# Sign of float64 weight slices from a Prelu on ScalarE, fp32r products in the first unit, and a new order, in an mLSTM-and-MLP kernel

## The chip, the cores and the metric

The kernel runs on one core of a Trainium2 chip. Its engines run side by side, each through its own queue in program order, and wait for one another by semaphores: TensorE (PE; its weight loads are PEld) multiplies into PSUM, VectorE (DVE) and ScalarE (ACT) do elementwise work, GpSimd (POOL) does a little of that on SBUF alone, and SyncE (SP) issues the DMAs. The metric is the device time of the program in microseconds, the median of several runs.

## The reference

Two stages. The first is a recurrent attention over 768 steps for 4 batches of 8 heads of width 40, with exponential gates that are kept stable by a running maximum `m`:

```
m_new  = max(f_t + m, i_t)
f_stab = exp(f_t + m - m_new);  i_stab = exp(i_t - m_new)
C = f_stab*C + i_stab * (v_t k_t^T)      # 40 x 40 per head
n = f_stab*n + i_stab * k_t
y_t = sigmoid(o_t) * (C q_t) / max(|n . q_t|, 1)
```

The second takes the 3072 x 320 result as `x`:

```
h = x @ w_in                     # 320 x 2048, float64
g = h * clip(h + 3, 0, 6) / 6
out = (g @ w_out) as float32     # 2048 x 320, float64
```

The weights come as float64, the rest as float32, and the result is float32.

## The kernel before

**Stages.** The recurrence is computed in chunks of 128 steps: inside a chunk it is a masked product of q, k and v, and between chunks a 40 x 40 state `C` is carried. Six chunks of 4 batches make 24 rows of 128 tokens; three of them are a unit, and eight units follow one another. A unit has two tasks (four heads each) of three chunks. Per chunk there are these jobs: `gate` (the matrix `gw` of gate weights: its first seven made by TensorE products `gb`, the others by a DMA from a scratch tensor and a masking on GpSimd, then four exponentials on ScalarE), `front` (scores `s`, times `gw` on VectorE, and the state's update), `back` (product `o` with v), and per task `fin` (division, output gate, transpose into `xh` and `xl`, the high and low part of x in fp32r). Then the unit's MLP: 16 slices `f` of 128 hidden columns. For each, `mm1` makes `h` by eight fp32r products, ScalarE and VectorE make `g`, and for each pair of slices `mm2` adds to three output tiles `acc`.

**Precision.** For units u >= NV, `g` is split into `gh` (cast on ScalarE, through the helper line L403) and `gl` (the rest, VectorE, L918), and the output weights into `vh` and `vl`, so that `mm2` makes three fp32r products per slice and tile (L937 to L939). Unit 0 (u < NV = 1) uses the whole fp32 `g` and the whole fp32 weight `vr` in one product (L935), which the profile shows as two instructions. For tasks >= PT = 6, `front` splits the weighted scores into three bf16 parts `p` (cast, subtract, cast, subtract) and `split_v` does so with v (`vb`), and `back` makes 16 bf16 products; the tasks before that use fp32 (L741).

**The weights.** The float64 words arrive as pairs of 32-bit words, eight slices of `w_in` (`rawi`) and eight of `w_out` (`rawo`). `weight_slice` makes the float32 value of each: ScalarE scales the high word, read as a float32, by 2^-112 (L824) and turns the low word into three bits (L826); then there are three operations on `y`, the clamp (L829), a shift with an OR of the low word's bits (L831), and an AND that takes the sign bit of the high word with an OR (L836). For `w_in`, `whi`, `wlo` and `wtl` are then split off for `mm1`. `split_out` makes `vh` and `vl`; it is set off for each slice by an `mm2` step of unit 0.

**The order.** Nothing is left to a run-time scheduler. A planner written in the kernel (class `Plan`) plays the jobs against a table of costs and due times, and writes each engine's queue in the order that it finds. The constants at the top are its due times and offsets (SPAN, T0, AH, EV, EG, MV, G0 to G2, ...), its cost corrections (BA, BD, BG) and buffer counts. `ENGINES` is a string with a letter for each of 28 choices: d, a or p for VectorE, ScalarE or GpSimd alone, x for VectorE or GpSimd, y for VectorE or ScalarE, z for all three. GP gives the groups of chunks in which the gates are computed, FC chooses how `fin` of unit 0 is cut. Until the `mm1` buffers are opened, the job `warm` puts filler products `pw` (128 x 128 bf16 of zeros) into TensorE's queue wherever the work of the last 3.41 us of the plan is below RATE columns.

Of the kernel before, what the change touches and what calls it, by code (L numbers as in the profile page):

```python
# [7 lines left out]
F32 = mybir.dt.float32  # L8
# [3 lines left out]
AF = mybir.ActivationFunctionType  # L12
ALU = mybir.AluOpType
# [18 lines left out]
MS = 1  # L32
BKO = 9.255
CHANGE = {"moe": 0.085, ("moe", "front"): 0.092, ("moe", "state"): 0.092, ("back", "front"): 0.085, ("fin", "front"): 0.095, ("back", "state"): 0.085, ("fin", "state"): 0.095, ("front", "moe"): 0.105, ("state", "moe"): 0.106}
STICK = 39.626
NGW = 3
NPT = 2
W_DOWN = 2.0**-112
W_MAX = 2.0**-96 * (1.875 - 2.0**-23)
W_LOW = 0.9374 * 2.0**-29  # L40
PT = 6
GB = 7
NV = 1
NY = 3
NRAW = 3
SPAN = 69.454
T0 = 103.209
AH = 21.763
GP = [1, 2, 3]
G0 = -113.271  # L50
G1 = -53.152
G2 = 54.685
AH1 = 87.929
FC = 1
FCS = {2: [[(0, 2)], [(0, 1), (1, 1)]], 3: [[(0, 3)], [(0, 2), (2, 1)], [(0, 1), (1, 1), (2, 1)], [(0, 1), (1, 2)]], 1: [[(0, 1)], [(0, 1)]]}
LON = 4.789
WAI = -1.158
WAO = -18.316
WAS = 151.09
MV = -6.903  # L60
DELTA = -1.652
EGW = 1
EV = 99.864
EG = 59.663
HOP = 0.167
# [280 lines left out]
def mlstm_moe_kernel(ctx: ExitStack, tc: tile.TileContext, ig, fg, qkd, natd, ond, w_in, w_out, ident_d, out):  # L346
    nc = tc.nc
# [18 lines left out]
    VR, VH, VL = {}, {}, {}  # L366
# [31 lines left out]
    def E(c):  # L398
        return {"d": nc.vector, "g": nc.gpsimd}[c]
# [413 lines left out]
    def weight_slice(kind, i, n):  # L813
# [9 lines left out]
        yield "a", 0.73  # L823
        nc.scalar.activation(w, hw.bitcast(F32), AF.Copy, scale=W_DOWN)  # L824
# [4 lines left out]
        E(e).tensor_scalar(w, w, W_MAX, -W_MAX, ALU.min, ALU.max)  # L829
        yield "d", Lock(0.765)  # L830
        nc.vector.scalar_tensor_tensor(lw, y, 3, lw, ALU.logical_shift_left, ALU.bitwise_or)  # L831
# [271 lines left out]
```

## Time and profile before

| | |
|---|---|
| median of 3 runs | 505.31 us (505.13 to 507.19) |
| the profiled execution | 505.4 us, span 503.7 us |
| granted TensorE clock | 0.999 |
| PE busy | 494.5 us (98%) |
| DVE busy | 356.1 us (71%) |
| ACT busy | 262.3 us (52%) |
| POOL busy | 95.2 us (19%) |
| first `h` product | 50.54 us |

A row of the profile names the line, the engine, the operation and the tiles as out<-in; "x128" is the number of instructions, then come their busy time and the mean duration of one in ns. In rows in order of time the first column is the start in us and the second the length. Matmuls are pipelined, and their durations overlap: what one costs is the distance between two starts, not its length. Line numbers after L403 differ by one or two between the two kernels, since one line was added at the top and two were taken out of `weight_slice`.

### The profile page before, as it was taken

How to read it: one execution, taken by the hardware profiler on the slowest of the kernel's cores; microseconds unless marked ns; L12 is line 12 of the kernel's file. 1: busy time of each engine (PE TensorE's matmuls, PEld its weight loads, DVE VectorE, ACT ScalarE, POOL GpSimd, SP SyncE). 2: the span in 40 equal slices, each digit the busy share in tenths (PEclk: the TensorE clock that was granted, in tenths of full speed). 3: DMA queues.
4: the chain of work that ended last, by engine and by line, in shares of the span. 5: the costliest groups of instructions: out<-in, count | busy, mean ns of one | idle time of the engine just before them, and what ended most of it. 6: DMA issues, size and time to landing. Idle time of an engine off the chain costs nothing.

```text
span 503.7 us, 10688 instructions
## 1 busy us (share of the span) xinstructions
PE 494.5 (98%) x4199; PEld 465.3 (92%) x4199; DVE 356.1 (71%) x839; ACT 262.3 (52%) x606; POOL 95.2 (19%) x117
## 2 busy tenths in 40 slices
PE   8999999999999999999999999999999999999997
PEld 7998787889999999999999999999899999999997
DVE  7998898976556676766877677777878777753332
ACT  4866758644456554555545554644545552343333
POOL 3213001001011141421233132421223131000000
PEclk9999999999999999999999999999999999999999
DMA  8757865514232231324131441324140230001001
GB/s 280 254 157 222 298 187 190 165 44 142 64 104 83 69 116 51 116 82 135 46 108 43 116 122 52 115 92 123 42 122 25 81 101 2 1 1 40 1 0 40
DMA packets 24610, 50.79 MB, mean 101 GB/s; under 512 B 2544, under 2 KB 9008, under 8 KB 24560
## 3 DMA queue, kind: packets, MB, share of 16 engines
q1 hardware_dynamic: 24560, 50.11, 31.8%
q8 instruction: 33, 0.54, 0.5%
q14 instruction: 17, 0.14, 0.1%
HBM read 46.07 MB, written 4.03 MB: 99 GB/s over the span
## 4 chain that ended last, share of the span: by engine, by line
PE 82%; DVE 5%; DMA 5%; ACT 3%; POOL 2%; issue 1%; POOLq 0%; SPq 0%; ACTq 0%; DVEq 0%
PE h L894 31%; PE acc L937 9%; PE acc L939 9%; PE acc L938 9%; PE s L693 5%; DMA gw<-gsc 5%; PE acc L935 4%; PE o L741 3%; PE s L696 3%; PE s L610 2%; PE x L798 2%; PE pw L424 1%; ACT gw L666 1%; PE o L743 1%; PE gb L654 1%
## 5 line engine op out<-in xcount | busy, mean ns | idle before, releaser
L908 ACT ACTIVATE g<-h,half 128x384 f32<-128x384 f32 x128 | 73.7, 576 | 109.3 <-PE h L894 101.9
L910 DVE SCALAR_TENSOR_TENSOR g<-g,h 128x384 f32<-128x384 f32 x128 | 70.6, 551 | 75.3 <-ACT g L908 74.7
L937 PE MATMUL acc<-vh,gh 128*128 128x320 f32 x336 | 106.9, 318 | 0.0
L939 PE MATMUL acc<-vh,gl 128*128 128x320 f32 x336 | 104.0, 309 | 0.0
L938 PE MATMUL acc<-vl,gh 128*128 128x320 f32 x336 | 103.9, 309 | 0.0
L894 PE MATMUL h<-xh,whi 128*128 128x384 f32 x256 | 92.3, 361 | 0.6 <-DVE g L910 0.5
L894 PE MATMUL h<-xh,wlo 128*128 128x384 f32 x256 | 86.5, 338 | 0.0
L894 PE MATMUL h<-xl,whi 128*128 128x384 f32 x256 | 86.4, 338 | 0.0
L918 DVE TENSOR_TENSOR gl<-g,gh 128x384 fp32r<-128x384 f32 x112 | 66.1, 593 | 20.9 <-ACT gh L403 19.6
L403 ACT CAST gh<-g 128x384 fp32r<-128x384 f32 x112 | 57.1, 510 | 44.0 <-DVE g L910 43.7
L666 ACT ACTIVATE gw<-gw,cT 128x128 f32<-128x128 f32 x164 | 54.2, 392 | 43.2 <-POOL gw L660 43.1
L660 POOL TENSOR_SCALAR_AFFINE_SELECT gw<-gw 128x512 f32<-128x512 f32 x41 | 29.4, 716 | 209.1 <-DMA gw<-gsc 140.9
L937 PEld LDWEIGHTS acc<-vh,gh 128*128 128x128 f32 x336 | 63.1, 188 | 0.5
L938 PEld LDWEIGHTS acc<-vl,gh 128*128 128x128 f32 x336 | 63.2, 188 | 0.0
L939 PEld LDWEIGHTS acc<-vh,gl 128*128 128x128 f32 x336 | 63.1, 188 | 0.0
L894 PEld LDWEIGHTS h<-xh,whi 128*128 128x128 f32 x256 | 48.1, 188 | 4.4 <-DVE g L910 2.8
L719 POOL TENSOR_TENSOR gw<-gw,p 128x512 f32<-128x512 f32 x30 | 35.0, 1166 | 85.7 <-DVE p L405 80.0
L894 PEld LDWEIGHTS h<-xl,whi 128*128 128x128 f32 x256 | 48.2, 188 | 0.6
L894 PEld LDWEIGHTS h<-xh,wlo 128*128 128x128 f32 x256 | 48.1, 188 | 0.0
L894 PE MATMUL h<-xh,wtl 128*128 128x384 f32 x128 | 43.3, 338 | 0.0
L894 PE MATMUL h<-xl,wtl 128*128 128x384 f32 x128 | 43.2, 337 | 0.0
L701 DVE TENSOR_TENSOR gw<-s,gw 128x512 f32<-128x512 f32 x48 | 32.9, 687 | 7.2 <-PE s L696 6.4
(112 smaller groups left out, 818.9 us busy)
## 6 DMA issues: line engine op xcount, KB each, us to landing
st<-in_qk_dram SPq DMA_DIRECT2D x48, 256.0 KB, 3.5
gw<-gsc SPq DMA_DIRECT2D x41, 256.0 KB, 3.3
nat<-in_nat_dram SPq DMA_DIRECT2D x16, 492.0 KB, 4.5
rawi<-in_w_in_dram SPq DMA_DIRECT2D x8, 640.0 KB, 6.4
rawo<-in_w_out_dram SPq DMA_DIRECT2D x8, 640.0 KB, 4.9
on<-in_on_dram SPq DMA_DIRECT2D x8, 480.0 KB, 4.5
out_dram<-ob SPq DMA_DIRECT2D x24, 160.0 KB, 1.8
f_s<-in_fg_dram SPq DMA_DIRECT2D x1, 96.0 KB, 2.2
```

The lines of the kernel that those rows point to most:

```text
L403: nc.scalar.copy(dst, src)
L660: nc.gpsimd.affine_select(gw, gw, pattern=[[0, 4], [1, L]], compare_op=ALU.is_ge, fill=NEG, base=0, channel_multiplier=-1)
L666: nc.scalar.activation(gw[:, h, :], src[:, h, :], AF.Exp, bias=cT[:, c, r0 + h : r0 + h + 1], scale=1.0)
L701: nc.vector.tensor_tensor(gw.rearrange("p (z j) l -> p z (j l)", z=2), sp[:, :, : 2 * L], gw.rearrange("p (z j) l -> p z (j l)", z=2), ALU ...
L719: E(e).tensor_sub(gw, gw, p[:, 0])
L894: nc.tensor.matmul(hp, w, x, start=n == 0, stop=n == len(seq) - 1)
L908: nc.scalar.activation(g, hp, AF.Relu, bias=half, scale=1.0 / 6.0)
L910: nc.vector.scalar_tensor_tensor(g, g, 1.0, hp, ALU.min, ALU.mult)
L918: E(e).tensor_sub(gl, g, gh.bitcast(F32))
L937: nc.tensor.matmul(acc, gh[:, ts_], VH[f // 4][:, f % 4, :], start=f == 0, stop=False)
L938: nc.tensor.matmul(acc, gh[:, ts_], VL[p][:, f % 2, :], start=False, stop=False)
L939: nc.tensor.matmul(acc, gl[:, ts_], VH[f // 4][:, f % 4, :], start=False, stop=f == NF - 1)
```

## The change

ScalarE's Copy of the high word becomes a Prelu with slope 2^32 for negative inputs. A negative weight then comes out 2^32 times as large in magnitude. That adds 32 to the exponent field, which is the bit 2^28 of the word, and the shift by 3 that follows anyway carries it into the sign bit. So the separate operation that fetched the sign (L836) is gone; the shift with OR writes the final tile, and the clamp has an asymmetric lower bound.

The constants: NV 1 to 0 (unit 0 uses the split fp32r form too, and `split_out` runs as soon as a slice of `w_out` is done), PT 6 to 4 (unit 2's tasks use the bf16 split), GP [1, 2, 3] to [1, 2, 1, 2], FC 1 to 0 (`fin` of unit 0 in one step of three chunks a task instead of two steps), RATE 4500 to 3690, and new due times. In ENGINES, among others, the subtractions of `p` and of v (23), the casts of `whi` (24) and the products `vp` (6) get other choices.

```diff
@@ constants
-BKO = 9.255
+BKO = 5.044
-STICK = 39.626
+STICK = 49.917
+W_SIGN = 2.0**32
-PT = 6
+PT = 4
-NV = 1
+NV = 0
-SPAN = 69.454
-T0 = 103.209
-AH = 21.763
-GP = [1, 2, 3]
+SPAN = 70.624
+T0 = 123.535
+AH = 19.252
+GP = [1, 2, 1, 2]
...
-FC = 1
+FC = 0
...
-RATE = 4500
+RATE = 3689.588
...
-ENGINES = 'ddpdddzxdaddxdddxxdaaaapaadx'
+ENGINES = 'dxpxadzddadddxddxxdaaaaxdapx'
@@ weight_slice
-        nc.scalar.activation(w, hw.bitcast(F32), AF.Copy, scale=W_DOWN)
+        nc.scalar.activation(w, hw.bitcast(F32), AF.Prelu, scale=W_DOWN, alpha=W_SIGN)
         yield "a", 0.73
         nc.scalar.activation(lw, lw, AF.Copy, scale=W_LOW)
         plan.now["t"] -= 0.73
         e = yield pick(14, d=Lock(0.46), g=1.0)
-        E(e).tensor_scalar(w, w, W_MAX, -W_MAX, ALU.min, ALU.max)
-        yield "d", Lock(0.765)
-        nc.vector.scalar_tensor_tensor(lw, y, 3, lw, ALU.logical_shift_left, ALU.bitwise_or)
+        E(e).tensor_scalar(w, w, W_MAX, -W_MAX * W_SIGN, ALU.min, ALU.max)
         fs = slice(i * 256, (i + 1) * 256)
         if kind == "o":
             VR[i] = wts.tile([128, 2, DM], U32, tag=f"vl{i}", bufs=1, name=f"vr{i}")
         yield "d", Lock(0.765)
-        nc.vector.scalar_tensor_tensor(VR[i].rearrange("p a d -> p (a d)") if kind == "o" else y, hw, 0x80000000, lw, ALU.bitwise_and, ALU.bitwise_or)
+        nc.vector.scalar_tensor_tensor(VR[i].rearrange("p a d -> p (a d)") if kind == "o" else y, y, 3, lw, ALU.logical_shift_left, ALU.bitwise_or)
```

Three places show how the queues move. The first is VectorE in the head of the program, from the first weight slice's clamp on (`yi` and `rawi` are the slice's tiles; the number after a name tells instances apart). Before:

```order
L829 TENSOR_SCALAR yi_166<-yi_166 128x640
L491 COPY cT<-pc_304 128x96
L831 SCALAR_TENSOR_TENSOR rawi_111<-yi_166,rawi_111 128x640
L495 COPY gTs<-pc_304 128x96
L836 SCALAR_TENSOR_TENSOR yi_166<-rawi_111 128x640
L577 TENSOR_TENSOR vp_146<-nat_107,wT 128x168
L829 TENSOR_SCALAR yi_175<-yi_175 128x640
L831 SCALAR_TENSOR_TENSOR rawi_112<-yi_175,rawi_112 128x640
```

Now:

```order
L830 TENSOR_SCALAR yi_166<-yi_166 128x640
L406 COPY ht_159<-o_0_312 128x168
L505 TENSOR_TENSOR wT<-pc_279,cT 128x32
L835 SCALAR_TENSOR_TENSOR yi_166<-yi_166,rawi_111 128x640
L492 COPY cT<-pc_336 128x64
L578 TENSOR_TENSOR vp_151<-nat_108,wT 128x168
L496 COPY gTs<-pc_336 128x64
L578 TENSOR_TENSOR vp_151<-nat_108,wT 128x168
L406 CAST whi<-yi_166 128x2x256
L578 TENSOR_TENSOR vp_369<-nat_150,wT 128x168
L830 TENSOR_SCALAR yi_175<-yi_175 128x640
```

One operation on 640 words stands after the clamp instead of two, and the `vp` products (GpSimd's before, but for one) and the cast of `whi` (ScalarE's before) have come into VectorE's queue.

The second is TensorE in unit 0, where the first `mm2` step begins. Before:

```order
L894 MATMUL h_2_1001<-xh_502,wtl 128x384
L894 MATMUL h_2_1001<-xl_503,wtl 128x384
L935 MATMUL acc_0_1029<-vr_660,g_0_974 128x320
L935 MATMUL acc_0_1029<-vr_660,g_1_997 128x320
L935 MATMUL acc_1_1036<-vr_660,g_0_974 128x320
L935 MATMUL acc_1_1036<-vr_660,g_1_997 128x320
L935 MATMUL acc_2_1045<-vr_660,g_0_974 128x320
L935 MATMUL acc_2_1045<-vr_660,g_1_997 128x320
L894 MATMUL h_3_1030<-xh_502,whi 128x384
```

Now, the first third of the step:

```order
L893 MATMUL h_4_964<-xh_540,wtl 128x384
L893 MATMUL h_4_964<-xl_541,wtl 128x384
L936 MATMUL acc_0_988<-vh_795,gh_0_865 128x320
L937 MATMUL acc_0_988<-vl_796,gh_0_865 128x320
L938 MATMUL acc_0_988<-vh_795,gl_0_866 128x320
L936 MATMUL acc_0_988<-vh_795,gh_1_915 128x320
L937 MATMUL acc_0_988<-vl_796,gh_1_915 128x320
L938 MATMUL acc_0_988<-vh_795,gl_1_916 128x320
L936 MATMUL acc_1_1006<-vh_795,gh_0_865 128x320
```

Three products take the place of one, and two more slices of `h` (up to 4 instead of 2) stand ahead of the first step.

The third is a chunk's split while unit 3's MLP runs (the first chunk of unit 4's second task). VectorE before:

```order
L405 COPY C_0_3253<-s_0_3183 128x84
L787 TENSOR_TENSOR on_2907<-on_2907,rd_0_3199 128x3x160
L405 CAST p_0_3263<-gw_0_2887 128x512
L910 SCALAR_TENSOR_TENSOR g_4_3247<-g_4_3247,h_4_3185 128x384
L918 TENSOR_TENSOR gl_4_3249<-g_4_3247,gh_4_3248 128x384
L804 TENSOR_TENSOR xl_3198<-x_8_0_3266,xh_3197 128x384
L405 CAST p_0_3263<-gw_0_2887 128x512
L723 TENSOR_TENSOR p_0_3263<-gw_0_2887,p_0_3263 128x512
L910 SCALAR_TENSOR_TENSOR g_5_3298<-g_5_3298,h_5_3246 128x384
```

VectorE now:

```order
L406 COPY C_0_3374<-s_0_3341 128x84
L406 CAST p_0_3442<-gw_0_3061 128x512
L720 TENSOR_TENSOR gw_0_3061<-gw_0_3061,p_0_3442 128x512
L406 CAST p_0_3442<-gw_0_3061 128x512
L805 TENSOR_TENSOR xl_3344<-x_8_0_3433,xh_3343 128x384
L724 TENSOR_TENSOR p_0_3442<-gw_0_3061,p_0_3442 128x512
L406 COPY ht_3340<-o_0_3464 128x168
L909 SCALAR_TENSOR_TENSOR g_5_3476<-g_5_3476,h_5_3404 128x384
```

The subtraction between the two casts of `p` (L720; L719 before) stood in GpSimd's queue and stands in VectorE's now, so the split no longer leaves that engine; in GpSimd's new queue, behind the gates' four subtractions, there is nothing but the maskings of `gw`.

More of the change, by code (lines that the diff above doesn't have):

```diff
@@ L39 @@
 W_MAX = 2.0**-96 * (1.875 - 2.0**-23)
+W_SIGN = 2.0**32
 W_LOW = 0.9374 * 2.0**-29
-PT = 6
+PT = 4
 GB = 7
-NV = 1
+NV = 0
 NY = 3
 NRAW = 3
-SPAN = 69.454
-T0 = 103.209
-AH = 21.763
-GP = [1, 2, 3]
[L50 to L53, printed above, removed]
-FC = 1
-FCS = {2: [[(0, 2)], [(0, 1), (1, 1)]], 3: [[(0, 3)], [(0, 2), (2, 1)], [(0, 1), (1, 1), (2, 1)], [(0, 1), (1, 2)]], 1: [[(0, 1)], [(0, 1)]]}
[L56 to L61, printed above, removed]
+SPAN = 70.624
+T0 = 123.535
+AH = 19.252
+GP = [1, 2, 1, 2]
+G0 = -120.578
+G1 = -25.639
+G2 = 24.583
+AH1 = 73.471
+FC = 0
+FCS = {2: [[(0, 2)], [(0, 1), (1, 1)]], 3: [[(0, 3)], [(0, 2), (2, 1)], [(0, 1), (1, 1), (2, 1)], [(0, 1), (1, 2)]], 1: [[(0, 1)], [(0, 1)]]}
+LON = -2.289
+WAI = 24.113
+WAO = -0.73
+WAS = 84.596
+MV = -25.163
+DELTA = -1.445
 EGW = 1
-EV = 99.864
-EG = 59.663
+EV = 127.005
+EG = 30.396
 HOP = 0.167
@@ L71 @@
 COLDX = 1.9
-RATE = 4500
+RATE = 3689.588
 WN = 128
-DELTA0 = 0.068
+DELTA0 = 0.131
 HOPP = 0.254
@@ L78 @@
 RATE_D = 300.0
-BL = 16.075
+BL = 7.052
 T_WARM = 6.9
 WGAP = 0.055
-ENGINES = 'ddpdddzxdaddxdddxxdaaaapaadx'
-BG = 0.605
-BA = 0.576
-BD = 0.79
+ENGINES = 'dxpxadzddadddxddxxdaaaaxdapx'
+BG = 1.587
+BA = -0.13
+BD = -0.329
 GS = 6
 FD = 2
-FIN0 = -79.361
+FIN0 = -97.197
 NE = 0
```

## The prediction

> **What bounds the kernel now.** I read the chain of waits first, then the busy times in stretches that I cut at the first `h` product of each unit (50.5, 110.1, 171.0 us and on), then what TensorE waited for.
>
> ```profile
> PE 82%; DVE 5%; DMA 5%; ACT 3%; POOL 2%; issue 1%; POOLq 0%; SPq 0%; ACTq 0%; DVEq 0%
> ```
>
> ```profile
> core 0: us, PE busy (x) PEld busy (x) DVE busy (x) ACT busy (x) POOL busy (x), PEclk, DMA share, GB/s
> 0.00:50.50 50.50, 47.46 (x616) 44.38 (x616) 42.86 (x128) 32.13 (x92) 12.88 (x23) 1.00 0.71 228
> 50.50:110.10 59.60, 58.11 (x365) 49.46 (x366) 54.01 (x113) 39.12 (x81) 4.74 (x7) 1.00 0.58 186
> 171.00:227.50 56.50, 56.50 (x498) 54.01 (x498) 40.64 (x96) 29.61 (x67) 16.07 (x18) 1.00 0.29 88
> 227.50:285.40 57.90, 57.56 (x515) 54.66 (x515) 43.60 (x104) 30.59 (x73) 14.86 (x16) 1.00 0.31 90
> ```
>
> ```profile
> PE x L798 <- DVE on L787: 1.9, 3, 1.2
> PE h L894 <- DVE g L910: 0.5, 1, 0.5
> ...
> L424 PE MATMUL pw<-ones 128*128 128x128 bf16 x270 | 19.0, 230 | 1.1 <-POOL ones L417 1.1
> ```
>
> From 50.5 us on TensorE is the bound: 58.1 of 59.6 us busy in unit 0, all of 56.5 in unit 2, and its longest waits sum to a few microseconds. In the head, before 50.5 us, "busy" misleads: 270 of its matmuls are filler (`pw`), 19.0 us that compute nothing. There VectorE (42.9 of 50.5) ends the waits. VectorE is also nearly full in unit 0 (54.0 of 59.6, 0.91), and has room only later (0.72 to 0.75). So a product saved pays at once, and VectorE work pays in the first 110 us.
>
> **The products.** Unit 0's second product now takes three fp32r products where it took one fp32 product of two instructions.
>
> ```profile
> 105.67 3.23 PE acc L935 x12
> 108.89 2.82 PE h L894 x16
> ...
> 454.79 0.31 PE L937 MATMUL acc<-vh,gh 128*128 128x320 f32 x1
> ...
> 457.29 0.31 PE L939 MATMUL acc<-vh,gl 128*128 128x320 f32 x1
> 457.44 0.34 PE L894 MATMUL h<-xh,whi 128*128 128x384 f32 x1
> ```
>
> One step of two slices and three tiles is 12 instructions and 108.89 - 105.67 = 3.22 us before; as 18 fp32r products it is 457.44 - 454.79 = 2.65. Eight steps: -4.6 us, seven of them (-4.0) inside unit 0's stretch.
>
> ```profile
> 25.70 0.89 PE o L741 x8
> 26.59 1.09 PE s L693 x16
> ...
> 201.78 0.21 PE L743 MATMUL o<-vb,p 128*128 128x84 bf16 x1
> ...
> 202.30 0.39 PE L937 MATMUL acc<-vh,gh 128*128 128x320 f32 x1
> ```
>
> PT 6 to 4 turns the `back` of unit 2's six chunks from fp32 (0.89 us) to the bf16 three-part form (16 matmuls, 0.52): 6 x 0.37 = -2.2 us. Together 6.8 us less for the engine that bounds.
>
> **The weight slices on ScalarE.** Prelu takes the place of Copy at equal shape and count; no row shows Prelu. Bounds: the Copy's own 0.80 us, and twice that, +0.8 x 16 = 12.8 us over the 110 us in which ScalarE is busy 71. I take 0.80, since operands and shape are the Copy's own; at the upper end ScalarE would stand at 84 of 110 and still hide it, save some wait at the head's end (up to 1 us).
>
> ```profile
> L824 ACT ACTIVATE yi<-rawi 128x640 f32<-128x640 f32 x8 | 6.4, 803 | 0.3 <-DMA rawi<-in_w_in_dram 0.3
> L480 ACT ACT_TABLE_LOAD x1 | 1.3, 1283 | 0.8 <-PEq L1089 0.8
> ```
>
> A table load before and after each Prelu would be 32 x 1.28 = 41 us, but the new ScalarE order holds one load, as the old. The Trainium skill (ScalarE: Activation LUTs, "Step-by-step: what each stage is for") says that an ACTIVATE passes one element per cycle whatever the function; by that rule, too, the term is zero.
>
> **VectorE in the head.** One slice loses a merge (L831 and L836 become one).
>
> ```profile
> 14.39 0.82 DVE L831 SCALAR_TENSOR_TENSOR rawi<-yi,rawi 128x640 uint32<-128x640 uint32 x1
> ...
> L405 DVE CAST p<-gw 128x512 bf16<-128x512 f32 x60 | 26.0, 434 | 15.3 <-POOL gw L719 15.3
> L852 DVE TENSOR_TENSOR wlo<-yi,whi 128x512 fp32r<-128x512 f32 x6 | 4.1, 683 | 0.0
> L577 DVE TENSOR_TENSOR vp<-nat,wT 128x168 f32<-128x168 f32 x11 | 3.5, 351 | 1.5 <-DMA nat<-in_nat_dram 0.9 <-POOL gw L660 0.6
> L403 ACT CAST gh<-g 128x384 fp32r<-128x384 f32 x112 | 57.1, 510 | 44.0 <-DVE g L910 43.7
> ...
> 173.90 0.55 DVE L918 TENSOR_TENSOR gl<-g,gh 128x384 fp32r<-128x384 f32 x1
> 174.37 0.68 DVE L701 TENSOR_TENSOR gw<-s,gw 128x512 f32<-128x512 f32 x1
> ```
>
> Back to back, an instruction costs its duration less 0.08 us (174.37 - 173.90 = 0.47 for one of 0.55). I price every instruction that the order lists so, with its duration beside an idle GpSimd. Up to the last `xl` before the first `h` product, the new VectorE order has four merges fewer (0.74 each, -2.9; a fifth `w_in` slice is through by then), less `wtl` work (-0.7), one chunk of `gw`, `ht` and `C` less (-1.6), the gates' subtraction of `m_s` on GpSimd (-0.9) and one `fin` step a task instead of two (-0.4). It gains that slice's clamp (+0.4), four `whi` casts (an estimate by L405: 0.35, +1.4), three `wlo` subtractions (+1.8) and six `vp` that were on GpSimd (+1.5). Together -1.4 us. The second gain is the GpSimd arithmetic that is gone:
>
> ```profile
> 40.95 0.61 DVE L849 TENSOR_TENSOR wtl<-yi,wtl 64x128 fp32r<-64x128 f32 x1
> 41.39 1.30 POOL L852 TENSOR_TENSOR wlo<-yi,whi 128x512 fp32r<-128x512 f32 x1
> 41.60 1.25 DVE L850 TENSOR_TENSOR wtl<-yi,wtl 64x128 fp32r<-64x128 f32 x1
> ...
> 44.84 0.48 DVE L829 TENSOR_SCALAR yi<-yi 128x640 f32<-128x640 f32 x1
> 45.48 1.22 DVE L831 SCALAR_TENSOR_TENSOR rawi<-yi,rawi 128x640 uint32<-128x640 uint32 x1
> ...
> 50.66 0.29 DVE L850 TENSOR_TENSOR wtl<-yi,wtl 64x128 fp32r<-64x128 f32 x1
> ```
>
> Beside a GpSimd instruction VectorE takes 0.61 and 1.25 where it takes 0.29 alone, and 1.22 for 0.82: 1.7 us in these three. Head: -1.4 - 1.7 = -3.1 us, if VectorE sets it. The other bound is the filler: 70 fewer at 2.18 / 39 = 0.056 each is -3.9, but how many are placed is also a rule of the planner (RATE) and no proof of less waiting. I take -3.1.
>
> ```profile
> 1.06 4.72 PE L424 MATMUL pw<-ones 128*128 128x128 bf16 x54 [1.06 <-POOL ones L417]
> ...
> 36.52 2.18 PE pw L424 x39
> ...
> 200.75 0.72 PE L693 MATMUL s<-st 64*128 64x128 f32 x8
> 201.30 0.54 PE L696 MATMUL s<-C,st 64*128 64x42 f32 x8
> ```
>
> The head's new `on` load and tanh ahead of the identity cast, and the gate subtraction on GpSimd, I cost at nothing: the first `gw` exponentials already stand behind that tanh, and the load is issued two places earlier; if it lands no sooner the cover is gone and the first `gb` waits about 2 us.
>
> One chunk of `s` and `o` moves from the head, where filler would have stood, to later, where TensorE is full: +1.9 us (201.30 - 200.75 and 201.78 - 201.30, and 0.89).
>
> **VectorE in unit 0.** By the same prices the stretch loses eleven merges (-8.1), `wtl` work (-1.5) and two `C` updates (-0.4), and gains 16 `gl` (+7.5), three `whi` casts (+1.0), three `vp` (+0.8) and the first splits of unit 2's `nat` and `gw` (+3.2): +2.5, from 47.8 to 50.3 us back to back. Before, it was busy 54.0, some 5.5 of it waiting on its own results, and idle 5.6. TensorE now needs 59.6 - 4.0 = 55.6; VectorE 50.3 + 5.5 and, from idle times that mostly close, 1.7: 57.5. So VectorE ends last here, +1.9 us. ScalarE gains 16 `gh` casts (0.51 each, 8.2 us on 39.1 of 57) and stays beneath.
>
> **VectorE later.** What GpSimd did goes to VectorE:
>
> ```profile
> L719 POOL TENSOR_TENSOR gw<-gw,p 128x512 f32<-128x512 f32 x30 | 35.0, 1166 | 85.7 <-DVE p L405 80.0
> L723 DVE TENSOR_TENSOR p<-gw,p 128x512 bf16<-128x512 f32 x30 | 20.7, 690 | 0.8
> L596 POOL TENSOR_TENSOR nat<-nat,vb 128x504 f32<-128x504 f32 x10 | 12.2, 1218 | 6.3 <-ACT vb L403 3.3 <-DVE vp L577 2.6
> ```
>
> 36 subtractions at 0.61 (the nearest row, L723), 12 of `nat` at about 0.6 and the `vp`: some 8 us a unit, 41 to 44 busy becomes 47 to 50 of 57, 0.85, between 0.75, where TensorE lost 0.3 us in unit 3, and unit 0's 0.91, where it lost 1.5. Over units 1 to 5 that is 0 to 5 us; against it the chunk's split gets shorter (0.69 for 1.17). I take +1.0.
>
> **Sum**, against the profiled execution's 505.4 us (span 503.7; the median is 505.31): -4.6 - 2.2 - 3.1 + 1.9 + 1.9 + 1.0 = -5.1, so **500.3 us**.
>
> **Rivals.** *VectorE keeps up everywhere.* For it: the GpSimd holds are gone, and 5.6 us of idle can close. Then TensorE's own account counts: products -6.8, filler -3.9 (the moved chunk nets to nothing, since filler gives way to it), and unit 0's 1.2 us wait on `on`: 505.4 - 6.8 - 3.9 - 1.2 = 493.5. *VectorE sets the first 110 us wholly.* For it: 0.85 and 0.91 busy. Its work up to unit 1's first product grows by 1.1 us (-1.4 + 2.5), and of GpSimd's holds 1.7 go in the head and, by GpSimd's busy time (4.74 against 12.88), 0.6 in unit 0. So unit 1 starts only 1.2 us earlier; with the moved chunk (+1.9), the eighth step (-0.6), `back` (-2.2) and +1.0 it is 504.3, no measurable change. Against it: the 5.6 us of idle. *Slower: the subtractions hold up the banks of `h`.* An `h` bank is free only when VectorE has multiplied `g`; now 36 chunks put two subtractions of 0.61 us more into the same queue than the casts alone. If TensorE waits half a subtraction (0.35 us) at each, 12.6 us, the sum without the other delay is 505.4 - 4.6 - 2.2 - 3.1 + 1.9 + 12.6 = 510. It outweighs the gain from 0.22 us a chunk on. Against it: six `g` buffers, and L910 held up `h` only once, for 0.5 us. *TensorE's clock falls.* 200 fillers, not 270, stand in the head. The granted clock is 1.00 in every stretch before, yet the first 54 fillers took 0.087 us each (4.72 / 54) and later ones 0.056, so a slower TensorE is there to be seen. If 10 us around the first `h` products ran at that rate, they would take 5.5 more: 500.3 + 5.5 = 506. The Trainium skill (TensorE: Matmul & The Clock Gate, "HAM oscillation — how this bites in real kernels") says that gaps of over about 3.4 us without matmuls drop the clock to half; the trace's clock of 1.00 with fillers neither shows nor denies it.
>
> **Chances.** Forecast 0.45 (its own range 497 to 503), keeps up 0.22, VectorE wholly 0.18, slower 0.10, clock 0.05. The range 492.5 to 506 leaves out under a tenth below and about a tenth above. One measurement tells 0.5%, 2.5 us: faster means under 502.8. Most of the forecast (0.42), all of "keeps up" and 0.06 of "wholly": 0.70; within 0.5%: 0.18; slower 0.12.
>
> **What would show it.** Right: the first `h` product at 46 to 48 us, unit 1's at 103 to 106; steps of 18 products at 2.65 us in unit 0; unit 0's stretch of 56 to 58.5 us with VectorE above 0.93; Prelu at 0.80 us; no VectorE row of 1.2 us. Wrong: unit 1 beginning at 108 or later (VectorE wholly); waits of `h` for `g` summing to over 5 us (the slower rival); a granted clock under 1.00; a Prelu row of 1.6 us.

## The result, and the profile after

The changed kernel takes **494.0 us** (median of four runs, 493.0 to 494.26) against 505.49 for the kernel before on the same chip: a ratio of 0.9763, 95% interval 0.9736 to 0.9789. It is faster by some 11.5 us. The forecast was 500.3 us, so the sign was right and the size was not: the gain is more than twice the 5 us that the sum gave. The profiled execution took 493.0 us, its span is 491.3.

The busy times of the changed kernel in stretches, cut at the first `h` product of a unit as before (the head, units 0, 1, 3 and 6):

```profile
core 0: us, PE busy (x) PEld busy (x) DVE busy (x) ACT busy (x) POOL busy (x), PEclk, DMA share, GB/s
0.00:44.16 44.16, 42.76 (x524) 39.71 (x524) 39.98 (x118) 30.93 (x86) 7.85 (x16) 1.00 0.72 238
44.16:101.07 56.91, 54.62 (x400) 51.88 (x400) 53.63 (x119) 45.92 (x100) 4.44 (x6) 1.00 0.63 203
101.07:160.18 59.11, 59.11 (x556) 56.49 (x554) 49.08 (x117) 29.47 (x67) 3.81 (x6) 1.00 0.28 88
...
218.64:275.44 56.80, 56.80 (x507) 54.66 (x506) 49.75 (x117) 29.53 (x70) 4.72 (x7) 1.00 0.32 97
...
390.81:441.04 50.23, 49.81 (x372) 48.31 (x371) 34.54 (x78) 20.77 (x44) 0.63 (x1) 1.00 0.04 12
```

The first `h` product comes at 44.16 us instead of 50.54, unit 1 begins at 101.07 instead of 110.14. So 6.4 us are gained in the head, 2.7 in unit 0 (56.91 for 59.60) and 3.3 in all that follows. VectorE has become fuller: 0.94 in unit 0, 0.83 and 0.88 in units 1 and 3. TensorE's longest waits show where that costs something:

```profile
PE h L893 <- DVE g L909: 2.2, 4, 0.8
PE pw L425 <- POOL ones L418: 1.1, 1, 1.1
PE x L799 <- DVE on L788: 0.4, 1, 0.4
```

The four waits of `h` for VectorE's `g` (2.2 us; before, there was one of 0.5 us) all lie in unit 0. Behind unit 0 the list has a single wait for VectorE, of 0.4 us, so there its higher share has cost TensorE no visible waiting.

To compare kernels I split TensorE's time from its first matmul on into three: the products at their price (the distance of two starts in an undisturbed row of the same form, times their count: for instance 0.175 us for an `h` product, 0.147 for an fp32r product of `acc`, 0.269 for each of the two instructions of an fp32 one), the filler at 0.056 us each, and the rest, which is lost to waiting or to a lower clock.

| us | products | filler | lost in the head | lost in unit 0 | lost later | first `h` |
|---|---|---|---|---|---|---|
| before | 461.6 | 15.1 | 5.6 | 3.1 | 17.2 | 50.54 |
| after | 454.9 | 11.2 | 4.9 | 4.9 | 14.4 | 44.16 |
| difference | -6.7 | -3.9 | -0.8 | +1.8 | -2.8 | -6.38 |

The rows behind the change's own terms, grouped by line and by engine (the Prelu by its shortest, median and longest duration in ns, with the first and the last start in us):

```profile
L425 PE MATMUL pw<-ones 128*128 128x128 bf16 x200 | 15.9, 242 | 1.1 <-POOL ones L418 1.1
L404 ACT CAST gh<-g 128x384 fp32r<-128x384 f32 x128 | 65.2, 511 | 47.8 <-DVE g L909 47.3
L917 DVE TENSOR_TENSOR gl<-g,gh 128x384 fp32r<-128x384 f32 x128 | 73.9, 579 | 9.6 <-ACT gh L404 8.0
L720 DVE TENSOR_TENSOR gw<-gw,p 128x512 f32<-128x512 f32 x36 | 25.4, 707 | 0.9
```

```profile
L825 ACT ACTIVATE yi<-rawi x8: 777/787/809, 10.8 to 69.6; 128x640 f32<-128x640 f32 x8
L825 ACT ACTIVATE yo<-rawo x8: 782/807/813, 27.3 to 90.9; 128x640 f32<-128x640 f32 x8
```

And nine products of unit 0's `mm2` in order of time, of which the first and the tenth start are shown: nine take 70.09 - 68.77 = 1.32 us, so a step of 18 takes 2.64.

```profile
68.77 0.31 PE L938 MATMUL acc<-vh,gl 128*128 128x320 f32 x1
...
70.09 0.31 PE L938 MATMUL acc<-vh,gl 128*128 128x320 f32 x1
```

**The end of the head**, as both kernels' timelines show it. The rows are the last product `o` of unit 0, its sum into `ht`, the first step of the division (`rd`), the output gate's multiplication on the engine that does it, the last `xh`, and the first `h`. Before:

```profile
38.54 1.04 PE L741 MATMUL o<-nat,gw 128*128 128x42 f32 x8
...
40.60 0.32 DVE L751 TENSOR_TENSOR ht<-ht,o 128x168 f32<-128x168 f32 x1
...
43.82 0.15 DVE L777 SCALAR_TENSOR_TENSOR rd<-ht 128x4 f32<-128x4 f32 x1
...
45.99 1.02 POOL L787 TENSOR_TENSOR on<-on,rd 128x160 f32<-128x160 f32 x1
...
49.74 0.27 ACT L802 CAST xh<-x 128x128 fp32r<-128x128 f32 x1 [0.23 <-PE x L798]
...
50.54 0.44 PE L894 MATMUL h<-xh,whi 128*128 128x384 f32 x1
```

After:

```profile
34.27 1.04 PE L742 MATMUL o<-nat,gw 128*128 128x42 f32 x8
...
35.34 0.33 DVE L752 TENSOR_TENSOR ht<-ht,o 128x168 f32<-128x168 f32 x1
...
36.34 0.18 DVE L778 SCALAR_TENSOR_TENSOR rd<-ht 128x12 f32<-128x12 f32 x1
...
38.63 0.64 DVE L788 TENSOR_TENSOR on<-on,rd 128x480 f32<-128x480 f32 x1
...
43.25 0.48 ACT L803 CAST xh<-x 128x384 fp32r<-128x384 f32 x1 [0.43 <-PE x L799]
...
44.16 0.44 PE L893 MATMUL h<-xh,whi 128*128 128x384 f32 x1
```

Of the 6.4 us, 4.3 are there before the output step begins: the last `o` starts at 34.27 instead of 38.54. By the account above, some 2.1 us of that are products (the chunk that has moved out) and 2.7 are filler (124 instead of 172 stand ahead of it); the waiting there is not less. The way from this `o` to `h` is 9.9 us instead of 12.0. `o` to `ht` takes 1.1 us where it took 2.1, and `ht` to `rd` 1.0 where it took 3.2 (VectorE had other work in between both times); from `rd` on it is 7.8 us, 1.1 longer than before, for a step of three chunks instead of one.

### The profile page after: what moved, and what is told of

Its sections match the earlier page's. It is cut to its first block, busy times and chain, and to the rows that moved or that the text cites. A ratio compares the mean times of both kernels' runs of the same rounds, so it can differ in the third digit from the quotient of the medians.

```text
span 491.3 us, 10775 instructions
## 1 busy us (share of the span) xinstructions
PE 484.1 (99%) x4227; PEld 463.7 (94%) x4227; DVE 392.5 (80%) x926; ACT 268.5 (55%) x618; POOL 34.1 (7%) x55
## 4 chain that ended last, share of the span: by engine, by line
PE 85%; DVE 6%; DMA 4%; ACT 2%; issue 1%; SPq 1%; POOL 0%; POOLq 0%; DVEq 0%; ACTq 0%
PE h L893 33%; PE acc L936 11%; PE acc L938 10%; PE acc L937 10%; PE s L694 5%; PE s L697 3%; PE s L611 2%; DMA nat<-in_nat_dram 2%; DMA gw<-gsc 2%; PE x L799 1%; PE pw L425 1%; PE o L744 1%; PE o L742 1%; PE o L746 1%; DMA st<-in_qk_dram 1%; PE gb L655 1%
## 5 line engine op out<-in xcount | busy, mean ns | idle before, releaser
L936 PE MATMUL acc<-vh,gh 128*128 128x320 f32 x384 | 122.1, 318 | 0.0
L938 PE MATMUL acc<-vh,gl 128*128 128x320 f32 x384 | 118.9, 310 | 0.0
L937 PE MATMUL acc<-vl,gh 128*128 128x320 f32 x384 | 118.8, 309 | 0.0
L404 ACT CAST gh<-g 128x384 fp32r<-128x384 f32 x128 | 65.2, 511 | 47.8 <-DVE g L909 47.3
L917 DVE TENSOR_TENSOR gl<-g,gh 128x384 fp32r<-128x384 f32 x128 | 73.9, 579 | 9.6 <-ACT gh L404 8.0
L936 PEld LDWEIGHTS acc<-vh,gh 128*128 128x128 f32 x384 | 72.1, 188 | 1.3
L937 PEld LDWEIGHTS acc<-vl,gh 128*128 128x128 f32 x384 | 72.2, 188 | 0.0
L938 PEld LDWEIGHTS acc<-vh,gl 128*128 128x128 f32 x384 | 72.1, 188 | 0.0
L661 POOL TENSOR_SCALAR_AFFINE_SELECT gw<-gw 128x512 f32<-128x512 f32 x41 | 27.9, 680 | 352.6 <-DMA gw<-gsc 208.4
L694 PE MATMUL s<-st 64*128 64x128 f32 x384 | 34.3, 297 | 0.3 <-DMA st<-in_qk_dram 0.3
```

Of the source, the lines that this page charges most:

```text
L404: nc.scalar.copy(dst, src)
L661: nc.gpsimd.affine_select(gw, gw, pattern=[[0, 4], [1, L]], compare_op=ALU.is_ge, fill=NEG, base=0, channel_multiplier=-1)
L694: nc.tensor.matmul(sp[:, z, hs], st[rows, 1, hs], st[rows, 0, hs], start=True, stop=True)
L917: E(e).tensor_sub(gl, g, gh.bitcast(F32))
L936: nc.tensor.matmul(acc, gh[:, ts_], VH[f // 4][:, f % 4, :], start=f == 0, stop=False)
L937: nc.tensor.matmul(acc, gh[:, ts_], VL[p][:, f % 2, :], start=False, stop=False)
```

## The experiments

Two views stood against each other throughout. In the one, each edit is worth what it takes off the engine that bounds, and the sum of the edits is the gain. In the other, the edits pay only together, since one spends the engine time that another frees, and the order decides. A third, which runs beside them, is that `fin` in one step a task carries the gain of the head. "Planned" means that the planner wrote the queues anew with the edit; "held" means that all queues keep the changed kernel's order and one kind of instruction alone is exchanged, added or left out, of which the planner knows nothing. Beside e1 to e4, e5 to e8, e9 to e12 and e13 to e15 the kernel before took 506.3, 506.3, 506.0 and 506.4 us (medians).

| run | time, us | ratio to before, 95% | products | filler | lost: head, unit 0, later | first `h` |
|---|---|---|---|---|---|---|
| e1 after with FC = 1 | 500.58 | 0.9859 to 0.9913 | 454.9 | 15.8 | 5.4, 5.1, 15.5 | 51.3 |
| e2 after with old ENGINES | 500.66 | 0.985 to 0.9938 | 454.9 | 14.0 | 4.5, 9.0, 17.7 | 46.6 |
| e3 before with Prelu | 506.39 | 0.998 to 1.0028 | 461.6 | 15.6 | 5.3, 4.9, 16.2 | 51.7 |
| e4 e3 with NV = 0 | 502.70 | 0.9901 to 0.9955 | 457.0 | 16.2 | 5.7, 3.8, 17.5 | 52.6 |
| e5 after, sign undone, held | 504.89 | 0.9943 to 1.0002 | 454.9 | 11.2 | 10.2, 10.0, 16.5 | 49.5 |
| e6 after, `p` on GpSimd, held | 499.31 | 0.9829 to 0.989 | 454.9 | 11.2 | 5.4, 4.7, 20.5 | 44.7 |
| e7 after with NV = 1 | 498.60 | 0.9832 to 0.9881 | 459.6 | 11.2 | 5.0, 4.6, 14.4 | 44.4 |
| e8 after with PT = 6 | 494.38 | 0.9752 to 0.98 | 457.2 | 11.2 | 4.9, 5.0, 13.6 | 44.2 |
| e9 after, sign undone, planned | 506.14 | 0.9986 to 1.0024 | 454.9 | 11.5 | 5.1, 13.5, 18.3 | 46.6 |
| e10 after, 133 fillers less, held | 500.25 | 0.9818 to 0.9921 | 454.9 | 3.8 | 14.7, 4.6, 15.2 | 46.6 |
| e11 before with FC = 0 | 510.28 | 1.0052 to 1.0104 | 461.6 | 14.2 | 9.5, 5.6, 17.6 | 53.5 |
| e12 after, `p` on GpSimd, planned | 497.46 | 0.9799 to 0.9858 | 454.9 | 11.2 | 5.1, 4.5, 18.7 | 44.4 |
| e13 after, `on` x `rd` on GpSimd, held | 494.86 | 0.9754 to 0.9799 | 454.9 | 11.2 | 6.5, 3.7, 16.4 | 45.8 |
| e14 e4 with FC = 0 | 503.58 | 0.9927 to 0.9984 | 457.0 | 16.1 | 6.2, 4.1, 16.0 | 51.2 |
| e15 after with GP = [1, 2, 3] | 497.37 | 0.9795 to 0.9848 | 454.7 | 12.0 | 5.6, 5.6, 16.6 | 45.6 |

The account is of the one profiled execution, the time is the median of all. The two lie over 2 us apart in e2 (the profiled execution took 502.96) and in e10 (495.9). In e2, e5, e9, e10 and e11 the granted clock of the profiled execution stood at half for some microseconds, and that time is in the lost columns.

**e1 and e2: two constants of the new kernel set back.**

```diff
-FC = 0
+FC = 1
```

> The changed kernel with FC = 1 again: fin of unit 0 in two steps a task instead of one. The planner then places 283 fillers in the head instead of 200. Theory V (VectorE's work sets the head, as predicted): one more fin step a task costs VectorE 0.4 us, so the first h product comes at 44.2 + 0.4 = 44.6 us and the time is 494.5. Theory F (the head is set by the turns PE, ScalarE, VectorE of fin and the transposes, of which two steps need twice as many): 83 fillers of 0.056 us, first h at about 48.8, time about 498.6.

```diff
-ENGINES = 'dxpxadzddadddxddxxdaaaaxdapx'
+ENGINES = 'ddpdddzxdaddxdddxxdaaaapaadx'
```

> The changed kernel with the old ENGINES string: the subtractions of p and nat, the vp products and some wlo on GpSimd again, whi cast on ScalarE. Theory V: VectorE has about 50 us less to do in all, but GpSimd's holds come back, 1.7 us in the head and 0.6 in unit 0; time about 496. Theory P (GpSimd as a slow link in the chains is what cost the kernel before, in the head and in units 1 to 7): 50 more fillers, first h at about 47, and the 2.4 us that units 1 to 7 gained beyond their products go too; time 499 to 500.

With two output steps a task again, the first `h` comes at 51.28 us, 7.1 later, behind 83 more fillers (+4.6 us) and 1.9 us more of products, and 6.6 us of the 11.5 are gone, more than either theory gave. With the old letters the first `h` comes 2.4 us later, and unit 0, where VectorE was fullest, loses 9.0 instead of 4.9. Part of that is the clock: in the profiled execution it stood at half for 6.8 us from 55.8 on, and the two executions at a full clock took 499.3 and 499.0 us. So the letters are worth about 5.1 us at a full clock, and 6.7 by the medians. Together with the products of NV (4.6, e7 below) the single losses come to 16 us and more, so they cannot be terms of one sum of 11.5.

What the letters moved is less than the section on the change and the expectation say: the letter of `vp` (6) is z in both strings, and in e2 `vp` stays on VectorE and ScalarE and `wlo` on VectorE. With the old letters GpSimd has only the first subtractions of `p` (36) and those of v (12) again, ScalarE the casts of `whi`, and VectorE the gates' subtractions.

**e3, e4 and e14: the edits that have a name, one by one, in the kernel before** (Prelu; then NV = 0 too; then FC = 0 too, with the old letters, due times and gate groups).

```diff
-        nc.scalar.activation(w, hw.bitcast(F32), AF.Copy, scale=W_DOWN)
+        nc.scalar.activation(w, hw.bitcast(F32), AF.Prelu, scale=W_DOWN, alpha=W_SIGN)
...
-        nc.vector.scalar_tensor_tensor(lw, y, 3, lw, ALU.logical_shift_left, ALU.bitwise_or)
...
-        nc.vector.scalar_tensor_tensor(VR[i].rearrange("p a d -> p (a d)") if kind == "o" else y, hw, 0x80000000, lw, ALU.bitwise_and, ALU.bitwise_or)
+        nc.vector.scalar_tensor_tensor(VR[i].rearrange("p a d -> p (a d)") if kind == "o" else y, y, 3, lw, ALU.logical_shift_left, ALU.bitwise_or)
```

> The kernel before with the Prelu edit alone (Prelu on ScalarE, one VectorE operation fewer per slice, old constants). Theory V: 16 x 0.74 = 11.8 us less for VectorE, some 4 of them in the head; first h at 46.5 to 47.5, time 501 to 502. Theory F: the turns are what they were (279 fillers against 270), first h at 50 to 51, time 504.5 to 506. Prelu rows stand at 0.80 us in either.

> The kernel before with the Prelu edit and NV = 0, other constants old. Both theories take 4.6 us off TensorE's products. Theory V: the head as with the Prelu alone, unit 0 bound by VectorE (16 gl more): about 500. Theory F: the head has 290 fillers, 20 more than before, +1.1 us; about 502.

> The kernel before with the three edits that a reader would name (Prelu for the sign, fp32r in unit 0, one output step a task in unit 0), with the old engines, the old due times and the old order of gates. If these three edits together are the gain, and only lack each other, the time is 497 or less. If the new placement and due times are needed to use the freed time, the time stays near that of Prelu with fp32r in unit 0 (502.7) or worse, 500 to 506: the queue holds 288 filler products against 200 in the changed kernel and 270 before, which is 16 us of filler, with 457 us of products and 27 to 32 lost.

Sixteen VectorE operations less, alone, are worth nothing (506.39, ratio 1.0004): the planner lays the queues out anew, the first `h` comes at 51.7, and what VectorE has free isn't asked for. NV = 0 on top gives 3.7 us, a little less than the 4.7 us of products that it saves. FC = 0 on top gives nothing more (503.58). So the three together are worth 2.8 us of 11.5. The rest needs the other constants: the letters, the gate groups, PT, RATE and the due times with the placement that follows from them.

**e5 and e9: the sign's own operation put back into the new kernel**, held (the planner unaware) and planned.

```diff
-        nc.scalar.activation(w, hw.bitcast(F32), AF.Prelu, scale=W_DOWN, alpha=W_SIGN)
+        nc.scalar.activation(w, hw.bitcast(F32), AF.Copy, scale=W_DOWN)
...
-        nc.vector.scalar_tensor_tensor(VR[i].rearrange("p a d -> p (a d)") if kind == "o" else y, y, 3, lw, ALU.logical_shift_left, ALU.bitwise_or)
+        nc.vector.scalar_tensor_tensor(lw, y, 3, lw, ALU.logical_shift_left, ALU.bitwise_or)
+        nc.vector.scalar_tensor_tensor(VR[i].rearrange("p a d -> p (a d)") if kind == "o" else y, hw, 0x80000000, lw, ALU.bitwise_and, ALU.bitwise_or)
```

> The changed kernel in its own order, with only the weight slices undone: Copy on ScalarE again and the sign's AND with OR on VectorE right behind the shift, 16 more VectorE operations of 0.74 us back to back, unknown to the planner. Theory V (VectorE full in head and unit 0): nearly all 11.8 us arrive at TensorE, first h about 4 us later, unit 1 about 10 later, time about 503 to 504. Rival (VectorE has slack to close, 4 us idle in the head and 3 in unit 0): about half arrives, time 498 to 500.

> The changed kernel with the weight slices undone as in the run before (Copy, shift with OR, then the sign's AND with OR), but now the planner knows of the 16 operations and makes the order with them (205 fillers against 200). If VectorE is full in the new order wherever these operations stand, about 5 us arrive, as in the run before without its fall of the clock: 499 to 500. If the planner finds room for them (the 0 us that the Prelu alone was worth in the old order): 494 to 495.5.

(The diff is e5's. In e9 the planner is told of the operation that comes back, and the clamp has its old bound.) The same sixteen operations that were worth nothing in the old order take nearly the whole gain with them in the new one: 504.89 held, and 506.14 planned, no different from the kernel before and worse than either expectation. What they free is spent by the others, as the new order has it: unit 0's sixteen `gl`, and the arithmetic that came over from GpSimd. In the held run's profiled execution the 16 x 0.74 = 11.8 us of VectorE work become 10.5 us on TensorE (5.3 in the head, 5.2 in unit 0); the busy times show where, with VectorE at 0.97 to 0.98 from 40 us on:

```profile
0.00:20.00 20.00, 18.29 (x206) 16.66 (x206) 16.34 (x56) 12.30 (x38) 6.26 (x14) 1.00 0.72 253
20.00:40.00 20.00, 18.30 (x181) 17.07 (x178) 17.72 (x45) 11.48 (x33) 0.00 (x0) 0.83 0.56 190
40.00:60.00 20.00, 18.30 (x207) 17.06 (x206) 19.61 (x45) 14.59 (x32) 3.19 (x4) 1.00 0.71 214
...
80.00:100.00 20.00, 18.17 (x113) 17.47 (x111) 19.67 (x40) 17.03 (x39) 1.49 (x2) 0.91 0.56 178
```

But part of that is not VectorE's work itself: the granted clock falls to 0.83 and 0.91 in two of these stretches. It stood at half for 6.8 and 3.4 us, which is up to 5 us of TensorE's time. Two of e5's ten executions had a mean granted clock of 1.00, and both took 502.5 us. So at a full clock the operations cost 8.5 of the 11.8 us, and the rest of the 10.9 that the median shows comes with the clock. In e9 the clock stood at half for the same 6.8 and 3.4 us, both in unit 0, where 13.5 us are lost; its execution with the highest clock (0.997) still took 505.64.

**e6 and e12: the first subtraction of `p` back on GpSimd**, held and planned. In e12 the letter takes the 12 subtractions of v along (14.0 us on GpSimd), so only e6 has the subtraction of `p` alone.

```diff
-            E(e).tensor_sub(gw, gw, p[:, 0])
+            nc.gpsimd.tensor_sub(gw, gw, p[:, 0])
```

> The changed kernel in its own order, with the first subtraction of p (36 of 128x512) on GpSimd again: 36 x 0.61 = 22 us less on VectorE, each 1.17 us on GpSimd instead of 0.69 on VectorE, plus holds. Theory P (units 1 to 7 gained since GpSimd left the chunk's chain): time rises by about 2, to 496. Rival (the gain of units 1 to 7 is from the order or from elsewhere): no change, 493.5 to 494.5, or a little less because VectorE has more room.

```diff
-ENGINES = 'dxpxadzddadddxddxxdaaaaxdapx'
+ENGINES = 'dxpxadzddadddxddxxdaaaapdapx'
```

> The changed kernel with the subtractions of p on GpSimd (letter 23 of ENGINES p again), planned so. In the held order this cost 5.3 us, all of it in units 2 to 6. If the planner can place the longer chain: 494 to 495.5. If GpSimd's 1.17 us and its holds stay on the path whatever the order: 497 to 499.

Both are slower, by 5.3 (2 were expected) and 3.5 us, and the loss stands behind unit 0 (lost later 20.5 and 18.7 for 14.4), although VectorE has less to do. The busy times of units 1 to 6, first the changed kernel and then e12:

```profile
101.07:441.04 339.97, 339.55 (x3017) 326.12 (x3016) 280.88 (x657) 173.40 (x396) 21.85 (x33) 1.00 0.26 81
```

```profile
100.90:445.15 344.25, 341.57 (x3016) 326.49 (x3015) 256.87 (x612) 172.32 (x393) 79.22 (x80) 1.00 0.27 80
```

VectorE is busy 24 us less, and the stretch is 4.3 us longer. The groups of instructions show why. In the changed kernel, then in e12, then in e6:

```profile
L406 DVE CAST p<-gw 128x512 bf16<-128x512 f32 x72 | 30.9, 430 | 0.6
```

```profile
L720 POOL TENSOR_TENSOR gw<-gw,p 128x512 f32<-128x512 f32 x36 | 43.7, 1213 | 74.0 <-DVE p L406 73.6 <-ACT gw L667 0.4
L406 DVE CAST p<-gw 128x512 bf16<-128x512 f32 x72 | 32.6, 453 | 18.9 <-POOL gw L720 18.9
```

```profile
L406 DVE CAST p<-gw 128x512 bf16<-128x512 f32 x72 | 32.1, 446 | 28.4 <-POOL gw L720 28.4
```

The second cast of `p` needs the subtraction, and stands in VectorE's queue. While GpSimd takes 1.21 us for it (VectorE 0.71), VectorE waits: 18.9 us in all with the planner's other work put in between, 28.4 in e6, 0.6 in the changed kernel. Per subtraction that is 0.53 us in e12 and 0.79 in e6, against the 0.71 us of VectorE's work that it saves. What is queued behind waits too, and TensorE for it: behind unit 0 its list has `h` waiting for `g` for 1.7 us in four places in e12, and in e6 `x` and `o` waiting for VectorE's `on`, `xl` and `p` for 3.5 us in seven, where the changed kernel has one wait of 0.4 us. That is 2 to 3 us of the loss; where the rest goes is not shown.

**e7 and e8: the two edits that save products, undone.**

```diff
-NV = 0
+NV = 1
```

> The changed kernel with NV = 1: unit 0 with whole fp32 products again, 200 fillers as now. TensorE: +4.6 us; VectorE: 16 gl fewer in unit 0, so the 2.3 us for which TensorE idled in unit 0 may go. If products pay at once: 494 + 4.6 - 2.3 = 496 to 498.6. If VectorE bound unit 0 (theory V): no change, 494.

```diff
-PT = 4
+PT = 6
```

> The changed kernel with PT = 6: unit 2's chunks in fp32 again, six times 0.37 us more on TensorE, and 6 chunks' splits fewer on VectorE. If the products pay at once: +2.2, time 496.2. If the splits on VectorE in units 0 and 1 hold TensorE up: no change or less, 493 to 494.

NV = 1 costs 4.6 us, just the 4.7 us of products, with the rest of the account as it was. That speaks for products that pay at once, and against theory V in unit 0: with 16 `gl` fewer VectorE is at 0.87 there (57.3 of 65.9 us), no `h` waits for `g` any more, and 4.6 us are lost all the same. The planner has put more of the later products into that stretch, so this is no clean test of the bound. PT = 6 costs 0.4 by the medians, with intervals that overlap; the products are 2.3 us more, and later losses 0.8 less, perhaps because the splits of six chunks are gone from VectorE and ScalarE. Between nothing and 2 us, this term stays open.

**e10: filler left out.** Only the first 67 fillers are issued; the 133 left out compute nothing for the result.

```diff
-            if "mo" not in plan.done:
+            if "mo" not in plan.done and plan.now["t"] < 8.0:
```

> The changed kernel in its own order without the fillers after the first 67 (133 fewer). If they only fill waits: no change, 494. If they delay products: up to 2 us less, 492. If they hold the clock up: the granted clock falls to 0.5 in the head for one or more stretches of 3.4 us, each of which costs up to 1.7 us, time 496 to 500.

The time is 6.3 us longer (500.25, 495.9 to 501.77; the profiled execution is the shortest of the four). The busy times of that execution:

```profile
10.00:20.00 10.00, 8.05 (x63) 6.82 (x63) 8.53 (x32) 8.18 (x30) 0.72 (x1) 0.83 0.81 296
20.00:30.00 10.00, 10.00 (x117) 9.29 (x117) 9.87 (x29) 7.50 (x20) 0.00 (x0) 1.00 0.54 181
30.00:40.00 10.00, 9.17 (x92) 8.44 (x90) 8.65 (x24) 6.01 (x18) 0.64 (x1) 0.78 0.71 242
40.00:50.00 10.00, 9.21 (x55) 8.60 (x54) 9.13 (x21) 7.77 (x21) 1.27 (x2) 0.53 0.66 210
```

The clock is at half for 3.4 us from 15.2 on and for 13.7 from 35.7 on, over the first `h` products. Up to 15.2 us, with the clock still full, 33 fillers (1.8 us) fewer stand before the mask product of `gb`, and it begins at 15.37 instead of 15.70, only 0.33 us sooner. So there the filler mostly fills waiting time, and with it the clock stays up. Behind 35.7 us the half clock hides what the missing fillers would have saved.

**e11: `fin` in one step, alone, in the kernel before.**

```diff
-FC = 1
+FC = 0
```

> The kernel before with FC = 0 alone (fin of unit 0 in one step a task), 254 fillers against 270. If fin's turns set the head's end in any order (theory F): 16 x 0.056 and the waits between, first h 1 to 2 us earlier, time 503.5 to 504.5. If one step is worth as much as it is in the new order (6.6 us): 499. If VectorE set it: 505.

It is slower, by 4.3 us: one step has to wait for the third chunk, and in the old order the head loses 9.5 us for 5.6, part of it again to a half clock (6.8 us from 50.4 on); the one execution at a full clock took 508.11, 2.1 us longer than the kernel before. In the new order the same edit is worth 6.6 (e1). The theory that `fin` in one step carries the head by itself falls, and none of the three expected times came true.

**e13 and e15: two parts of the head.** In e13 the multiplication of `on` by `rd` in unit 0's two output steps is GpSimd's.

```diff
-        E(e).tensor_tensor(of, of, rd.rearrange(
+        (nc.gpsimd if u == 0 else E(e)).tensor_tensor(of, of, rd.rearrange(
```

> The changed kernel with every queue's order held, but the multiplication of the output by 1/n (on times rd) in the two output steps of unit 0 runs on GpSimd, where the old kernel had it for one of them, instead of VectorE. Open is why the head ends 6.4 us earlier than before. If the way from the last product o to the first h (9.9 us in the changed kernel, 12.0 before) is set by VectorE's and GpSimd's places at its end, each of the two steps gets longer by the difference of the two durations: 0.64 us on VectorE, and an estimate of 1.0 to 1.5 us on GpSimd by the old kernel's rows (1.02 for 128x160, 1.22 for 128x504), so the first h comes at 44.7 to 45.5 us and the time is 494.5 to 495.5. If GpSimd's part there was the main cost of the old head, the first h comes at 46.5 or later and the time is 496.5 or more. If it is hidden by the wait for the bank of the second transposition, nothing moves: 44.2 us and 494.

```diff
-GP = [1, 2, 1, 2]
+GP = [1, 2, 3]
```

> The changed kernel with the old grouping of the gates (1, 2, 3 chunks instead of 1, 2, 1, 2), planned anew. The queue holds 215 filler products instead of 200. If the grouping only moves a little work in the head: 494 to 496 (15 fillers are 0.8 us). If the early gates of unit 0's third chunk are what lets the last product o stand 4.3 us earlier: the first h at 47 or later, and 497 or more.

In e13 the multiplication takes 0.99 us and begins late, since the masking of `gw` stands ahead of it in GpSimd's queue:

```profile
40.61 0.64 POOL L661 TENSOR_SCALAR_AFFINE_SELECT gw<-gw 128x512 f32<-128x512 f32 x1 [1.91 <-DMA gw<-gsc]
...
41.22 0.99 POOL L788 TENSOR_TENSOR on<-on,rd 128x480 f32<-128x480 f32 x1
...
42.26 0.55 PE L799 MATMUL x<-ident,on 128*128 128x128 f32 x3 [0.56 <-POOL on L788]
...
45.81 0.44 PE L893 MATMUL h<-xh,whi 128*128 128x384 f32 x1
```

The first `h` comes 1.65 us later, but 0.89 of that is older than the edit: `s` waits 1.2 us for its input's DMA at 8.9 us, and from there on every product stands 0.89 later up to 40.7 us. The edit itself costs 0.76 us in the head. The time is 0.9 longer, with intervals that overlap; unit 0's stretch is 55.8 us instead of 56.9, and loses 3.7 instead of 4.9, so that something other than the first `h` sets its end. So GpSimd's place at the head's end is a small part of the 6.4 us. The gate groups are a larger one: with the old groups the time is 3.4 us longer, 1.4 of them in the head (45.57), the others behind it; the first `h` at 47 or later did not come true.

## Why the prediction was wrong in its size

**The products (forecast -6.8 us): right.** The account gives -6.7; e7 confirms the larger term (4.6). A step of 18 products takes 2.64 us, as forecast.

**The Prelu at 0.80 us: right.** The rows show 0.79 and 0.81 at the median, and the Copy that it replaced had a mean of 0.803. That agrees with the Trainium skill (ScalarE: Activation LUTs, "Step-by-step: what each stage is for"), by which one element passes per cycle whatever the function.

**Unit 0 (forecast: VectorE ends last, +1.9, stretch of 57.5 us, above 0.93): right in its numbers, and its cause shown in part.** The stretch is 56.91 us with VectorE at 0.94, and 1.8 us more are lost. All waits of TensorE in its list there are for VectorE's `g`, but they are 2.2 of the 4.9 us lost, and e7 loses 4.6 without them. In e5, VectorE work added to the head and unit 0 delays TensorE.

**The head (forecast -3.1, and +1.9 for the chunk that moves out of it: -1.2): this step failed.** The head's part of the account is -4.7 (filler -3.9, lost -0.8), and the first `h` at 44.16 and unit 1's at 101.07 lie outside the forecasts of 46 to 48 and 103 to 106. That VectorE no longer slows down beside GpSimd's arithmetic came true (its longest row is 1.03 us). Two things were mis-sized. VectorE's limit was made by counting its rows up to the last `xl`, and the single output step a task came out of that at -0.4; yet what lies between two dependent instructions in the queues counts, and not the row alone. The last `o` comes 4.3 us earlier, and `rd` follows `ht` after 1.0 us instead of 3.2; undoing the one step delays the first `h` by 7.1 us and costs 6.6 (e1). Which of the places brings how much is not shown. The "other bound", 70 fillers less, was read off the order and set aside since RATE might have made it; it was the right one (-3.9), and e1 shows that fillers follow the placement (83 more at the same RATE). And the moved chunk was put down as +1.9, on the assumption that its place in the head would only be filled with filler. The head lost the chunk's products (27.1 us there for 28.8) and 70 fillers besides, so it got shorter by the chunk's whole time, and the move cost nothing.

**Later units (forecast +1.0): this step failed too, in sign.** 2.8 us less are lost. VectorE's higher share was priced as waiting, and the shorter split only named beside it. The higher share costs one wait of 0.4 us in TensorE's list behind unit 0. The shorter split is what pays: with the subtraction of `p` on GpSimd the held order loses 5.3 us (e6), and with those of v besides a planned one loses 3.5 although VectorE has 24 us less to do (e12). A queue that crosses to another engine and back stands still meanwhile, and what stands behind in it comes late.

These two steps are 3.5 + 3.8 = 7.3 us, which is the distance from the sum (500.3) to the profiled execution (493.0).

**The rivals.** "VectorE keeps up everywhere" (493.5) is nearest. It has the products, the filler and the moved chunk right, but that it hits the time is partly luck: it has unit 0 losing 1.2 us less, where 1.8 more are lost, and leaves out the 0.8 and 2.8 us that the head and the later units gain, and these errors nearly cancel. "VectorE sets the first 110 us wholly" wanted unit 1 at 108 or later; it begins at 101.07. "The subtractions hold up the banks of `h`" wanted waits of over 5 us; they are 2.2. The falling clock isn't there (1.00 in all stretches), but in five of the experiments it is.

**What stays open.** The losses when single parts are set back (medians: 12.1 for the sign, 6.7 for the letters, 6.6 for FC, 4.6 for NV, 3.4 for the gate groups) sum to nearly three times the gain; those of the sign and the letters contain some microseconds of a half clock. In the planned runs, part of each is that the due times were chosen for the whole; what a newly tuned order without that part would reach wasn't tried. Nor were RATE and the due times changed alone.

## What to carry to other kernels

An edit that frees an engine which isn't the bound can be worth nothing (here 0 of 11.8 us of VectorE work) until other work is moved into the freed place, and then it is worth what that work saves: price the edits of one change together, and test one by undoing it in the new kernel as well as by doing it in the old. To price a new order, compare the places of the instructions on the path (what stands between two dependent ones) rather than sums of durations; filler that disappears from the bounding engine's queue can be a sign of shorter waits. A short operation on another engine in the middle of a chain makes the first engine's queue wait for the whole crossing.

## What the runs showed of the hardware

In the profiled executions of e2, e5, e9, e10 and e11 the granted clock falls to half in the head or unit 0, for 3.4 us or a multiple (6.8, 13.7), where TensorE has waited a little more; no single wait passed 3.0 us. In e9, TensorE in order of time:

```profile
75.39 0.34 PE L895 MATMUL h<-xl,wtl 128*128 128x384 f32 x1
77.90 0.52 PE L799 MATMUL x<-ident,on 128*128 128x128 f32 x3 [2.17 <-DVE on L788]
...
81.33 0.52 PE L895 MATMUL h<-xh,wtl 128*128 128x384 f32 x1
81.64 0.52 PE L895 MATMUL h<-xl,wtl 128*128 128x384 f32 x1
```

```profile
78.30:85.10 6.80, 5.90 (x21) 4.95 (x20) 6.77 (x13) 6.80 (x21) 0.00 (x0) 0.50 0.42 120
```

After a wait of 2.17 us the `h` products are 0.31 us apart instead of 0.175, and the clock is at half for 6.8 us. The Trainium skill (TensorE: Matmul & The Clock Gate, "HAM oscillation — how this bites in real kernels") speaks of gaps of over some 3.4 us; here falls came with shorter ones (3.0 us in e2, 2.17 in e9, 2.07 and 0.75 in e11), and in e10 behind waits of 0.35 to 0.56 us one after another. The length of a wait alone does not decide: one of 1.83 us at 94.3 us in e5 was followed by no fall. So a wait of 2.2 us cost up to another 3.4 (half of 6.8), and a kernel whose filler is placed by a plan can lose that cover when the plan is off.
